# Splitting the prologue's fills over three engines and its LayerNorm into four batches, in a fused attention and GeGLU kernel

## The chip, the cores and the metric

The kernel runs on one core of a Trainium2 chip. The metric is the device time of one execution in microseconds (us). Each kernel was executed several times, and one execution was taken with the hardware profiler. Before the change the three timed executions gave a median of 945.88 us (945.6 to 949.18).

Engines are named as the profile names them: PE is TensorE, PEld its weight loads, ACT is ScalarE, DVE is VectorE, POOL is GpSimd, SP is SyncE, which issues the transfers.

## The reference

```python
x = A_x                                          # [1, 2048, 640], bf16
h = x + attention(layernorm(x), wqkv, wo)        # 32 heads of 20, softmax over 2048 keys
h2 = h + geglu(layernorm(h), w_gate, w_up, w_down)   # inner width 1728
```

The LayerNorm has neither scale nor shift, only (x - mean) / sqrt(var + 1e-5). The softmax needs 32 x 2048 x 2048 exps.

## The kernel before

Nearly all of the time is exps: ScalarE takes most of them, VectorE computes the rest by bit tricks. Ahead of the first exp stands a **prologue**. It loads x, computes the first LayerNorm ("LN1") over 16 tiles of 128 rows, transposes the result on TensorE, projects the first K rows and Q rows, bounds the scores with a maximum over K, and only then starts. This change concerns the prologue.

The program does not write the order of its instructions. It lists operations with a duration, a priority (a smaller number goes first) and what they read and write. A list scheduler in the program turns this into one fixed order for each engine before anything runs:

```python
def op(self, eng, fns, dur, prio, reads=(), writes=(), acq=(), rel=(), after=(), sem=None, lat=None, ...):
...
P_QK, P_PV, P_EPI, P_BG = 0, 1, 2, 3
...
def load(dst, src, key, mb, after=(), writes=None):
    return op("sp", I("dma_start", dst, src), 0.08, P_BG, ..., sem=key, lat=2.2 + mb / 0.25)
```

So `dur` and `lat` are what the scheduler believes. They cost nothing themselves, but a wrong belief gives a bad order, and on the chip an engine stands at the first instruction in its order that can't start: in the run with the fills alone below, TensorE stood 1.94 us at a V matmul, until 17.18, and transposes whose input was ready at 15.98 ran at 19.00.

K and Q are laid out with padding rows that have to be filled first. All the large fills are on Pool:

```python
fills(0, 1, 0, 1)            # K group 0 (1024 words), Q chunk 0 group 0 (256)
... constants ...
fills(1, NG, 0, 1)           # K groups 1 to 7 in one: 7168 words; Q chunk 0: 1792
for c in range(1, 4):        # Q chunks 1 to 3, 2048 words each
    cst(I("memset", qt_all[:, c, :, :]..., 0.0), "qtm%d" % c, 256 * NG)
op("dve", I("memset", PS[:, 512 * 6:512 * 7], 0.0), 0.6, P_QK, ...)
op("dve", I("memset", v_all[:, :, :, DH:DH + 1], 1.0), 0.6, P_QK, writes=["vones"])   # one bf16 in every 21
```

LN1 goes in batches of 4, 4 and 8 tiles. For each tile VectorE takes the statistics (two bn_stats and a bn_aggr). For each batch a few small operations and a square root on ScalarE give the reciprocal deviation. Then each tile is normalised (the "apply"), transposed on TensorE into PSUM (`ps` in the profile), and copied out by ScalarE (the "evacuation"):

```python
for t0, n, eng in ((0, 4, "act"), (4, 4, "act"), (8, 8, "dve")):
    for t in range(t0, t0 + n):
        ln_stats(x_sb[:, t, :], t, [f"x{t // 4}"], P_BG)
    ln_rsqrt(t0, n, P_EPI, True)
    for t in range(t0, t0 + n):
        e_ops.append(ln_apply(eng, x_sb[:, t, :], xn_p[:, t % 4, :], ("xnp", t % 4), t, ...))   # four buffers
        transposes(xn_p[:, t % 4, :], ..., xnT[:, :, t * 128:(t + 1) * 128], ("xnT", t), ALLB, P_EPI, "act")
```

## Time and profile before

| part of the span | us | bounded by |
|---|---|---|
| prologue, to the first exp | 41.46 | LN1, then the K and Q projection |
| exps | 850.18 | ScalarE, busy 842.66 of it |
| tail, from the table load behind the last exps | 52.26 | the last tiles' work, in a chain |
| span | 943.9 | |

The first exp and the tail's table load are read from ScalarE's timeline, and the tail is the difference to the span. Three more lines of the same profile matter later, from VectorE's timeline. The columns are start, duration, engine, line, operation, output and input, and in brackets the idle time before it and what ended that.

```profile
0.98 0.48 DVE L339 MEMSET ps<- 128x512 f32 x1 [0.98 <-PEq L1134]
3.31 0.48 DVE L339 MEMSET v_all<- 128x512 bf16 x1 [1.84 <-issue]
5.14 0.49 DVE L339 BATCH_NORM_STATS2 stats<-rege 128x6 f32<-128x320 bf16 x1 [1.34 <-DMA rege<-in_A_x_dram]
```

The memset of single ones has a gap of 1.84 us in front of it that no wait explains ("issue"). Here it costs nothing, because the statistics wait for x until 5.14 anyway. What the gap is, is worked out with the profile after.

### The profile page before, as it was taken

What the parts mean: (1) busy time and instruction counts of PE and PEld (TensorE: products, weight loads), DVE (VectorE), ACT (ScalarE), POOL (GpSimd) and SP (SyncE); (2) the same over time, 40 slices, a digit from 0 to 9 for tenths busy, and PEclk for the clock granted to TensorE, in tenths of its full rate; (3) what the DMA queues carried; (4) which work ended last, traced back from release to release, by engine and by line L of the source; (5) the groups of instructions that cost most, each with busy time, mean ns of one, the idle gap of its engine ahead of it and who ended that gap; (6) DMA issues with size and microseconds to landing.
All of it is one profiled execution on the core that took longest, in us unless ns stands there. A gap on an engine that the chain in (4) does not pass through costs nothing.

```text
span 943.9 us, 23617 instructions
## 1 busy us (share of the span) xinstructions
PE 852.4 (90%) x10332; PEld 367.6 (39%) x10388; DVE 829.6 (88%) x1804; ACT 881.4 (93%) x789; POOL 17.9 (2%) x26
## 2 busy tenths in 40 slices
PE   2999999998898999998898997999999899999998
PEld 1533232222232223232243333344434446566577
DVE  8849999999799997988799999798999989989953
ACT  3799999999999999999999999999999999999931
POOL 7000000000000000000000000000000000000000
PEclk9999999999999999999999999999999999999999
DMA  7121102325500000001000000001100000000000
GB/s 250 51 73 35 52 15 67 92 59 156 181 1 1 1 1 1 1 15 42 1 3 1 2 1 1 1 2 30 30 1 2 2 15 18 3 17 10 3 22 16
DMA packets 22047, 30.13 MB, mean 32 GB/s; under 512 B 1964, under 2 KB 19464, under 8 KB 21944
## 3 DMA queue, kind: packets, MB, share of 16 engines
q1 hardware_dynamic: 21944, 28.63, 9.8%
q8 instruction: 81, 1.33, 0.6%
q14 instruction: 22, 0.18, 0.1%
HBM read 20.12 MB, written 8.09 MB: 30 GB/s over the span
## 4 chain that ended last, share of the span: by engine, by line
ACT 70%; PE 17%; DVE 12%; issue 0%; DMA 0%; DVEq 0%
ACT pts L339 45%; ACT rege L339 24%; PE ps L592 4%; DVE rege L339 4%; PE ps L1006 4%; PE ps L829 3%; PE ps L339 2%; PE ps L1057 2%; DVE rege L789 2%; DVE qt_all L339 2%; ACT L339 1%; DVE regw L622 1%; DVE stats L339 1%; PE ps L556 1%; DMA rege<-in_A_x_dram 0%
## 5 line engine op out<-in xcount | busy, mean ns | idle before, releaser
L339 ACT ACTIVATE pts<-ps 128x1536 bf16<-128x1536 f32 x480 | 572.2, 1368 | 8.4 <-PE ps L829 5.1
L829 PE MATMUL ps<-qt_all,kt_all 32*128 32x256 bf16 (+2 forms) x3584 | 304.0, 289 | 47.4 <-ACT pts L339 29.2
L339 ACT ACTIVATE rege<-ps 128x1536 bf16<-128x1536 f32 x239 | 298.9, 1369 | 1.7 <-PE ps L339 1.6
L829 PEld LDWEIGHTS ps<-qt_all,kt_all 32*128 32x128 bf16 x3584 | 96.0, 92 | 274.6 <-ACT pts L339 161.4
L339 DVE TENSOR_TENSOR qt_all<-qt_all 128x1024 bf16<-128x1024 bf16 (+1 forms) x240 | 164.1, 684 | 3.2
L1006 PE MATMUL ps<-rege,regw 128*128 128x256 bf16 (+2 forms) x955 | 146.4, 287 | 12.8 <-ACT rege L339 4.8
L339 PE MATMUL ps<-pts,v_all 128*21 128x256 bf16 (+2 forms) x2098 | 138.8, 290 | 0.9 <-DVE rege L339 0.5
L789 DVE TENSOR_SCALAR rege<-ps 128x512 int16<-128x512 f32 x154 | 105.4, 684 | 30.1 <-PE ps L829 29.1
L339 DVE TENSOR_SCALAR qt_all<-qt_all 128x1024 bf16<-128x1024 int16 (+1 forms) x288 | 115.6, 418 | 2.0
L339 PE MATMUL ps<-rege,v_all 128*21 128x256 bf16 (+2 forms) x1294 | 113.3, 292 | 0.0
L1006 PEld LDWEIGHTS ps<-rege,regw 128*128 128x128 bf16 x980 | 72.8, 98 | 63.4 <-issue 21.2
L592 PE MATMUL ps<-regw 128*128 128x320 bf16 (+1 forms) x342 | 81.5, 348 | 3.5 <-ACT regw L562 0.8
L1057 PE MATMUL ps<-regw,rege 128*128 128x320 bf16 x448 | 78.0, 301 | 1.9 <-DVE rege L1046 0.8
L339 PE MATMUL ps<-kt_all,zer 128*32 128x512 bf16 x824 | 70.6, 384 | 0.1
L789 DVE TENSOR_SCALAR qt_all<-ps 128x512 int16<-128x512 f32 x96 | 65.6, 685 | 3.2 <-PE ps L829 2.2
L339 DVE TENSOR_SCALAR rege<-rege 128x1024 int16<-128x1024 int16 (+2 forms) x166 | 67.3, 422 | 1.0
L339 DVE TENSOR_TENSOR rege<-rege 128x1024 bf16<-128x1024 bf16 (+3 forms) x103 | 66.1, 644 | 1.0
L339 PEld LDWEIGHTS ps<-pts,v_all 128*21 128x21 bf16 x2098 | 50.2, 91 | 38.4 <-issue 30.3
L1057 PEld LDWEIGHTS ps<-regw,rege 128*128 128x128 bf16 x448 | 36.9, 98 | 32.6 <-issue 15.2
L339 PEld LDWEIGHTS ps<-rege,v_all 128*21 128x21 bf16 x1294 | 41.1, 91 | 19.8 <-issue 14.3
L592 PEld LDWEIGHTS ps<-regw 128*128 128x128 bf16 x360 | 29.0, 98 | 45.9 <-issue 21.2
L1046 DVE TENSOR_TENSOR rege<-rege,ps 128x512 bf16<-128x512 bf16 (+1 forms) x53 | 35.8, 677 | 10.5 <-PE ps L1006 9.7
(86 smaller groups left out, 611.4 us busy)
## 6 DMA issues: line engine op xcount, KB each, us to landing
rege<-in_A_x_dram SPq DMA_DIRECT2D x6, 640.0 KB, 5.1
q_rows<-regw SPq DMA_DIRECT2D x20, 128.0 KB, 1.7
out_dram<-rege SPq DMA_DIRECT2D x16, 160.0 KB, 2.1
regw<-in_B_w_gate_dram SPq DMA_DIRECT2D x1, 2160.0 KB, 10.4
regw<-in_B_w_up_dram SPq DMA_DIRECT2D x1, 2160.0 KB, 15.4
regw<-in_B_w_down_dram SPq DMA_DIRECT2D x1, 2080.0 KB, 20.6
kt_all<-k_rows SPq DMA_DIRECT2D x12, 160.0 KB
qt_all<-q_rows SPq DMA_DIRECT2D x12, 160.0 KB
```

Source lines behind the costliest of these rows:

```text
L339: return lambda eng: getattr(eng, method)(*args, **kwargs)
L556: op("pe", lambda eng, a=a: eng.transpose(bank16(bk, D)[:, 128 * a:128 * a + 128], src[:, a * 128:(a + 1) * 128], ident[:]), 0.055, prio, ...
L592: yield op("pe", lambda eng, l=l, r=r, k=k: eng.matmul(bank(bk, n), l, r, start=(k == 0), stop=(k == len(steps) - 1)), c_mm(n), prio, mode ...
L622: e = op("dve", lambda eng: eng.tensor_copy(dst, bank(bk)), c_dve(512), prio, reads=[key], writes=[dkey], rel=[bk], after=after)
L789: d_ops.append(op("dve", lambda eng: eng.tensor_scalar(v[:, 512 * h:512 * h + 512], bank(b), EXP_MUL, -32000.0, ALU.mult, ALU.max), c_dve( ...
L829: return lambda eng: eng.matmul(out()[:, kk * nq:(kk + 1) * nq], kt_all[32 * j:32 * j + 32, g, kt * 128:(kt + 1) * 128], qt_all[32 * j:32 ...
L1006: op("pe", lambda eng, a=a, f=f, fi=fi: eng.matmul(bank(bk)[:, fi * nq:(fi + 1) * nq], w[:, a, F0[f]:F0[f] + 128], hnT[:, a, 128 * tb:128 ...
L1046: hdone.append(op("dve", lambda eng, bu=bu, fv=fv, w=w: eng.tensor_tensor(fv, fv, bank(bu, w), ALU.mult), c_dve(w), p, reads=[ku, ("ha", k ...
L1057: op("pe", lambda eng, f=f, o=o, hf=hf, bk=bk: eng.matmul(bank(bk, 320), ha_f[:, o:o + 128], wd[:, f, hf * 320:(hf + 1) * 320], start=(f = ...
```

## The change

The intent is to get the first exp earlier. The padding fills are spread over ScalarE, VectorE and Pool, in the time in which x still arrives, and Pool's are cut into small pieces. LN1 goes in four batches of four. The sums of the second batch are taken by ScalarE as the accumulated outputs of a Copy and a Square; all applies go to VectorE; two evacuations move to VectorE. A priority class P_PRO is added, for LN1 and for the first K and Q rows, and the square roots get a higher priority on ScalarE. Last, the scheduler's beliefs on when the loads land are set to later, more truthful times (also for wo's load and four weight loads under the exps, not shown): V's weights landed at 17.1 us in the runs below, where the old belief was 5.4.

```diff
-P_QK, P_PV, P_EPI, P_BG = 0, 1, 2, 3
+P_QK, P_PV, P_PRO, P_EPI, P_BG = 0, 1, 1.5, 2, 3
...
+        op("act", I("activation", nm[:, 0:1], zer[:, 0:2].bitcast(FP32), ACT.Sqrt), 1.5, P_QK, ...)
+        op("act", I("activation", f32(qt_all[:, 1, :, :]), zer[...].to_broadcast([128, 2048]), ACT.Copy), 1.8, P_QK, ...)
+        op("act", I("activation", f32(qt_all[:, 2, :, :]), zer[...].to_broadcast([128, 2048]), ACT.Copy), 1.8, P_QK, ...)
+        op("dve", I("memset", f32(kt_all[:, 1:4, :]), ones2), 2.9, P_QK, writes=["kf0"])
+        cst(I("memset", kt_all[:, 0, :].bitcast(FP32), ones2), "ktm0", 1024)
...
+        for g in range(4, NG):
+            cst(I("memset", kt_all[:, g, :].bitcast(FP32), ones2), "kf%d" % g, 800)
...
+        for g in range(1, NG, 2):
+            cst(I("memset", f32(qt_all[:, 0, g:min(g + 2, NG), :]), 0.0), "qf0%d" % g, 512)
...
-        fills(1, NG, 0, 1)
-        for c in range(1, 4):
-            cst(I("memset", qt_all[:, c, :, :]..., 0.0), "qtm%d" % c, 256 * NG)
+        for g in range(0, NG, 2):
+            cst(I("memset", f32(qt_all[:, 3, g:g + 2, :]), 0.0), "qf3%d" % g, 512)
...
-                      sem=key, lat=2.2 + mb / 0.25)
+                      sem=key, lat=mb)
-                 f"x{i}", 0.65)
+                 f"x{i}", 5.1 + 1.8 * i)
-        load(wqk, ..., "wqk", 1.6)
-        load(wv, ..., "wv", 0.8)
+        load(wqk, ..., "wqk", 14.0)
+        load(wv, ..., "wv", 16.4)
...
-        for t0, n, eng in ((0, 4, "act"), (4, 4, "act"), (8, 8, "dve")):
+        def act_stats(t0, n):
             for t in range(t0, t0 + n):
-                ln_stats(x_sb[:, t, :], t, [f"x{t // 4}"], P_BG)
-            ln_rsqrt(t0, n, P_EPI, True)
+                for f, k in ((ACT.Copy, 0), (ACT.Square, 1)):
+                    op("act", I("activation", junk, x_sb[:, t, :], f, accum_out=asum[:, k, t - t0:t - t0 + 1]), 0.86, 1.4, ...)
+            ... three small DVE operations turn the sums into mean and variance ...
+        for t0 in (0, 4, 8, 12):
+            if t0 == 4:
+                act_stats(4, 4)
+            else:
+                for t in range(t0, t0 + 4):
+                    ln_stats(x_sb[:, t, :], t, [f"x{t // 4}"], 1.4 if t0 == 12 else P_BG)
+            ln_rsqrt(t0, 4, P_PRO, sqrt=True)
+            for t in range(t0, t0 + 4):
+                e_ops.append(ln_apply("dve", ..., P_PRO))
+                transposes(..., P_PRO, "dve" if t in (13, 15) else "act")
...
-        proj_k(0, PRO, P_EPI, "act")
-        proj_q(0, 0, PRO, P_EPI, "act")
-        q_bound0(PRO, P_EPI)
+        proj_k(0, PRO, P_PRO, "act")
+        proj_q(0, 0, PRO, P_PRO, "act")
+        q_bound0(PRO, P_PRO)
...
-            proj_v(kt, 0, (6, 7), P_BG, "dve")
+            proj_v(kt, 0, (6, 7), P_EPI if kt < 4 else P_BG, "dve")
```

## The prediction

What the recorded texts call a wait for the port, or a port wait, is a VectorE instruction that lasts until a fill of Pool ends. In the profile before, a cast of eight numbers takes 2.73 us and ends at 12.10, as Pool's fill ends at 12.08; after Pool's last fill (19.31) a cast of sixteen takes 0.17. The times are measured. That a shared port is the cause was not shown.

> **What bounds the kernel now.** I read the page's overview first, then the table of engine busy time by stretch, then the timeline of each engine over the first 45 us, and last the waits of ScalarE. The overview has ScalarE (ACT) busy 93% of a 943.9 us span and 70% of the chain that ended last. The stretches say where the other 7% lies:
>
> ```profile
> core 0: us, PE busy (x) PEld busy (x) DVE busy (x) ACT busy (x) POOL busy (x), PEclk, DMA share, GB/s
> 0.00:41.46 41.46, 24.27 (x178) 14.36 (x181) 34.06 (x100) 22.15 (x34) 17.29 (x25) 1.00 0.47 159
> 41.46:100.00 58.54, 56.42 (x431) 18.60 (x437) 44.25 (x94) 58.27 (x52) 0.00 (x0) 1.00 0.19 57
> ...
> 400.00:500.00 100.00, 88.99 (x981) 32.49 (x986) 86.76 (x180) 100.00 (x89) 0.00 (x0) 1.00 0.05 15
> ```
>
> ScalarE is full from 41.46 us, where the first exp starts, to about 892 us, where the last one ends; the hundreds between 100 and 900 us show it busy 97.8 to 100.0 of 100. So the kernel is a prologue of 41.5 us, some 850 us of exps without a real gap, and a tail of about 52 us (the chain of the end has the last exps ending at 891.6 us). The change touches almost only the prologue. The question is therefore one number: how much earlier does the first exp start? Each microsecond there should come off the end, if the exps stay gapless.
>
> In the prologue the VectorE (DVE) timeline shows the loss:
>
> ```profile
> 6.00 6.08 POOL L339 MEMSET kt_all<- 128x7168 f32 x1
> ...
> 9.37 2.73 DVE L339 CAST mv<-mv 128x8 bf16<-128x8 f32 x1
> ...
> 12.13 7.18 POOL L339 MEMSET qt_all<- 128x1792 f32 x4
> 12.14 1.61 DVE L339 TENSOR_SCALAR sd<-mv 128x4 bf16<-128x4 bf16 x1
> ...
> 13.78 0.20 ACT L339 ACTIVATE sd<-sd 128x4 bf16<-128x4 bf16 x1 [11.70 <-DVE stats L339]
> ...
> 17.51 1.83 DVE L339 TENSOR_SCALAR sd<-mv 128x4 bf16<-128x4 bf16 x1
> ```
>
> Columns: start, time, engine, line, operation. A cast of eight numbers takes 2.73 us and ends at 12.10, just as Pool's fill, which began at 6.00, ends (12.08). The same cast takes 0.165 us at 25.25 us, when Pool has finished. And ScalarE does nothing but a table load until 13.78. The later part:
>
> ```profile
> 26.97 1.08 ACT L619 ACTIVATE regw<-ps 128x512 bf16<-128x512 f32 x2
> ...
> 29.20 4.88 ACT L562 ACTIVATE regw<-ps 128x640 bf16<-128x640 bf16 x8 [0.56 <-PE ps L556]
> 33.89 1.17 ACT L619 ACTIVATE regw<-ps 128x512 bf16<-128x512 f32 x2
> 35.47 0.60 ACT L619 ACTIVATE regw<-ps 128x512 bf16<-128x512 f32 x1 [0.41 <-PE ps L592]
> 36.09 1.28 ACT L339 ACT_TABLE_LOAD   x1
> 41.46 3.71 ACT L339 ACTIVATE pts<-ps 128x1536 bf16<-128x1536 f32 x3 [4.09 <-PE ps L829]
> ```
>
> LN1's last eight tiles wait for one late batch of eight. Their evacuations run until 34.1, the fourth K chunk is evacuated at 36.07, then come the maximum over K and the query bound on VectorE and TensorE (5.4 us), then the first exp. The exp table load is hidden in that gap.
>
> [...] the bn_stats keep their 0.44 us during Pool's fill, the cast and the tensor_scalar wait. [...] the trace has 0.70 for the evacuations and 0.913 for the ScalarE applies. [...] The trace has 0.48 us for 512[...].
>
> **The change, part by part.**
>
> *Fills.* Pool's 6.08 us and four 1.6 to 1.8 us fills go. VectorE writes three K groups (3072 words): [...] in a stretch (0.98 to 5.14) where it works 0.97 us in all. With the two old memsets [...] free, but with no slack. ScalarE writes two Q chunks of 2048 words: [...] behind a warm-up Sqrt; also free. Pool keeps pieces of 1024 words (0.95 us seen) and 512 (about 0.55, between 0.31 for 256 and 0.95). By my count of its list, 4.8 us for five K pieces, about 4.8 for the Q pieces and about 4 for the constants, it is done near 14 us instead of 19.3. [...]
> What this takes away on VectorE: the four stuck instructions lost 2.57 + 1.45 + 0.57 + 1.67 = 6.3 us against their free 0.16. What I put back: 1.5 us, some five waits of 0.3.
>
> *LN1.* VectorE loses four tiles of statistics: 4 x 0.86 = 3.4 us (one tile runs from 6.44 to 7.30). It gains eight applies at 0.37 (eight take 2.94 us): 2.9; two evacuations at about 0.4: 0.8; one more root group and three small operations on the sums: about 0.9, less the three products for the negative mean. Sum: -3.4 + 2.9 + 0.8 + 0.8 = +1.1. With the port: -6.3 + 1.5 + 1.1 = -3.7. Smaller batches remove the idle 1.15 us before the last reciprocal and some waits around it, say 1.5: about -5. The last apply, which ends at 31.0 now, should end near 26 to 27.
> ScalarE loses eight applies (7.0 us busy) and two evacuations, and gains eight sum passes of 640 [...] in the stretch from x1's landing to about 14 us that was empty. The x loads take about 1.7 us each (640 KB at about 380 GB/s), so x1 is there near 6.9. From 14 it has 14 evacuations at 0.61 (4.88 for eight), 5 K and Q evacuations at 0.53 and the small roots: 8.5 + 2.7 + 0.6 = 11.8, to about 26. Both engines come out level at 26 to 27, which is the mark of a balanced split, and also means that neither has slack for the other.
>
> *To the first exp.* Last evacuation about 27.5 (34.1 before), fourth K chunk evacuated about 29.5 (36.07). From there to the first exp: 5.4 us before, of which two K evacuations of 0.6 and one V evacuation of 0.4 were interposed in the maximum; the new priority class between attention and epilogue should keep most of them out, so 4.0 to 5.0. First exp near 34, a gain of 7.5; I add 0.5, because the V evacuations that I left in my VectorE count may be put off. About 8 us.
>
> **The rest of the kernel.** The exps, their count and the tail's work stay. But the program order comes from a list scheduler fed with these durations and landing times, so changed loads and keys can reshuffle the whole order. Between 100 and 900 us ScalarE is idle only about 7.3 us in sum, so a reshuffle can gain little there and lose some; the tail may move by 2 us either way. V work no longer done in a shorter prologue goes under the exps, where TensorE is 96% busy, partly with fillers that can give way. So 945.9 - 8 = 938.
>
> **Rivals.** First, *only the wait's place changes*: VectorE stays the bound of the prologue, with port waits at each of the first applies, because they are tensor_scalar and Pool still fills until about 14 us. For it: they are the form that got stuck. Against: pieces are short. Gain then 3 to 5, time 941 to 943. Second, *ScalarE becomes the bound*: if the accumulator costs a further 0.25 us a pass, or Square asks for another table (1.28 us for a load here, twice), evacuations begin 2 to 5 us later. The time is then 940 to 943. Third, *the DMA queue*: SyncE needs 0.74 us an issue (four take 2.96), so eight issues plus landing put the first K and Q rows near 26 if K is ready at 18; that hides, but not if the Q issues stand behind three K chunks. Gain then about 6. Fourth, *full success*: no interposing, all port waits hidden: the first exp at 31, time near 935. Fifth, *wash-out*: the first exp comes early, and ScalarE has new gaps waiting for V or for the second group's K. For it is only TensorE's 96%; against it, the second group's rows are issued by 53.8 us, some 15 us before their use. Time 940 to 945.
>
> **Range and chances.** The centre is 938. The rivals that lose leave 941 to 943, full success with a lucky tail 933. So 933 to 942.5. Faster by 2% would need the end below 927, a gain of 19 us out of a prologue where x lands until 10.3 and the QK weights until 14.6: 0.02. Slower by 2% would take a broken order: 0.01. Within 2%: 0.97.
>
> **What would show it.** In the changed profile: no VectorE instruction of eight numbers above about 1 us; ScalarE busy from about 1 to 14 us; Pool finished near 14; the first evacuation near 14 (16.47 before); the last near 27.5; the first exp between 31 and 36; then a stretch of exps as long as before (850 us) and a tail of about 52. I am wrong if the first exp moves by less than 5 us, if the table is loaded more than once before the exps, or if the exp stretch grows by more than 2 us.

## The result, and the profile after

The four executions of the changed kernel gave 938.92 us in the median (937.99 to 940.96), and the four of the kernel before on the same chip 945.84 (945.6 to 949.18). The ratio is 0.992 (95% interval 0.989 to 0.995). All ratios here are the mean time of one kernel's fast runs over that of the other's fast runs of the same rounds, so not quite the ratio of the medians that are quoted. By the 2% rule the verdict is "same"; against the kernel before alone it is a gain of 7 us.

The profiled execution was the slowest of the four. I took the unchanged changed kernel again in the first experiment job and got a second profile, in an execution of 938.21 us; its four times have a median of 938.39, and the ratio is 0.991 (0.990 to 0.993). The two profiles tell more together than either alone:

| us | before | changed, 1st profile | changed, 2nd profile |
|---|---|---|---|
| first exp starts | 41.46 | 36.40 | 35.22 |
| from there to the tail's table load | 850.18 | 851.05 | 849.48 |
| tail | 52.26 | 51.75 | 51.80 |
| span | 943.9 | 939.2 | 936.5 |

Of the 7.4 us by which the second profile is shorter, 6.24 are the earlier first exp, 0.70 the stretch of exps and 0.46 the tail. The stretches, first profile:

```profile
core 0: us, PE busy (x) PEld busy (x) DVE busy (x) ACT busy (x) POOL busy (x), PEclk, DMA share, GB/s
0.00:36.40 36.40, 21.84 (x154) 12.47 (x154) 30.28 (x97) 24.58 (x45) 12.15 (x32) 1.00 0.54 182
36.40:100.00 63.60, 60.13 (x481) 20.06 (x482) 48.75 (x103) 63.03 (x56) 0.00 (x0) 1.00 0.17 48
...
200.00:300.00 100.00, 91.88 (x791) 27.72 (x788) 94.15 (x213) 98.53 (x88) 0.62 (x1) 0.98 0.32 97
```

The prologue is 5 us shorter, with Pool busy 12.15 us in it and not 17.29. The last line shows where this execution is slower later: the granted TensorE clock was 0.98 there, and ScalarE stood idle for 1.47 us. In the second profile the same hundred has a clock of 1.00 and ScalarE busy 99.92. That is 1.39 of the 1.57 us by which the two stretches of exps differ; that the clock is the cause is likely, but not tested.

**The fills.** VectorE's timeline, first profile:

```profile
1.51 2.62 DVE L339 MEMSET kt_all<- 128x3072 f32 x1 [1.51 <-PEq L1155]
4.23 0.48 DVE L339 MEMSET ps<- 128x512 f32 x1
6.56 0.48 DVE L339 MEMSET v_all<- 128x512 bf16 x1 [1.84 <-issue]
6.66 1.22 DVE L339 BATCH_NORM_STATS2 stats<-rege 128x6 f32<-128x320 bf16 x3
...
10.57 0.15 DVE L339 CAST mv<-mv 128x8 bf16<-128x8 f32 x1
...
11.04 0.15 DVE L339 TENSOR_SCALAR sd<-mv 128x4 bf16<-128x4 bf16 x1
...
21.17 0.18 DVE L339 RECIPROCAL rs<-sd 128x4 f32<-128x4 bf16 x1 [1.32 <-ACT sd L339]
```

The cast of eight numbers takes 0.15 us at 10.57, where the kernel before took 2.73. Pool is then at its small constants, and its fills end at 14.58. The long waits at Pool's fills are gone. But the gap of 1.84 us before the memset of ones has moved. It now follows two other memsets, x has been there since 5.1, and the statistics start at 6.66 and not at 5.14. The last line is a new wait: VectorE stands 1.32 us for a root on ScalarE.

The gap is probably the memset's own time, for the row of a memset seems to begin late. VectorE's first instruction is the memset of 512 words in the kernel before, with a row from 0.98 to 1.46, and the one of 3072 words here, with a row from 1.51 to 4.13. If both began at the same moment (ScalarE's first row is at 0.80 in both), the 2560 further words took 4.13 - 1.46 = 2.67 us, or 1.04 ns each, where the lengths of the rows give (2.62 - 0.48) / 2560 = 0.84. In the same way the memset of ones has a row until 7.04, although the statistics begin at 6.66. From 4.71, where the memset before it ends, to 6.66 it would take about 1.95 us. Both figures are estimates from these rows.

**ScalarE.** Its timeline, first profile:

```profile
2.20 3.69 ACT L339 ACTIVATE qt_all<-zer 128x2048 f32<-128x2048 f32 x2
6.92 0.74 ACT L339 ACTIVATE rege<-rege 128x640 bf16<-128x640 bf16 x1 [1.04 <-DMA rege<-in_A_x_dram]
7.57 0.19 ACT L339 ACTIVATION_READ_ACCUMULATOR rege<-rege 128x1 f32 x1
...
15.67 1.88 ACT L568 ACTIVATE regw<-ps 128x640 bf16<-128x640 bf16 x3
20.45 0.60 ACT L641 ACTIVATE regw<-ps 128x512 bf16<-128x512 f32 x1 [2.90 <-PE ps L614]
20.94 0.29 ACT L339 ACTIVATE sd<-sd 128x4 bf16<-128x4 bf16 x2
...
24.57 4.88 ACT L568 ACTIVATE regw<-ps 128x640 bf16<-128x640 bf16 x8
...
30.82 0.60 ACT L641 ACTIVATE regw<-ps 128x512 bf16<-128x512 f32 x1 [0.39 <-PE ps L614]
31.43 1.28 ACT L339 ACT_TABLE_LOAD   x1
36.40 4.62 ACT L339 ACTIVATE pts<-ps 128x1536 bf16<-128x1536 f32 x4 [3.68 <-PE ps L850]
```

The fills and the sums are as planned, and there is no further table load between 2.09 and 31.43. After the fourth evacuation (17.55) ScalarE stands for 2.90 us, until the first K chunk comes from TensorE. Only behind that evacuation, in ScalarE's fixed order, come the roots of the second and third batch, and VectorE's applies wait for them. TensorE at that time, first profile and then second, each from its own timeline:

```profile
17.05 5.93 PE L614 MATMUL ps<-regw 128*128 128x320 bf16 x21 [0.46 <-ACT regw L568]
```

```profile
17.14 4.66 PE L614 MATMUL ps<-regw 128*128 128x320 bf16 x21 [0.55 <-DMA regw<-in_A_wqkv_dram]
```

The same 21 matmuls (V and K projections) took 5.93 us in one execution and 4.66 in the other. ScalarE, second profile:

```profile
19.73 0.60 ACT L641 ACTIVATE regw<-ps 128x512 bf16<-128x512 f32 x1 [2.19 <-PE ps L614]
...
35.22 4.62 ACT L339 ACTIVATE pts<-ps 128x1536 bf16<-128x1536 f32 x4 [3.68 <-PE ps L850]
```

Up to 17 us the two executions agree to within 0.1 us. Then the K evacuations come 0.72 us (the first) and 1.18 us (the second) earlier, and the first exp 1.18 us earlier.

### The profile page after: what moved, and what is told of

It reads as the page before. It is cut to its first block, busy times and chain, and to the rows that moved or that the text cites. A ratio compares the mean times of both kernels' runs of the same rounds, so it can differ in the third digit from the quotient of the medians.

```text
span 939.2 us, 23514 instructions
## 1 busy us (share of the span) xinstructions
PE 860.0 (92%) x10297; PEld 365.5 (39%) x10297; DVE 829.1 (88%) x1807; ACT 883.7 (94%) x799; POOL 12.8 (1%) x33
## 4 chain that ended last, share of the span: by engine, by line
ACT 77%; PE 15%; DVE 8%; issue 1%; DVEq 0%
ACT pts L339 50%; ACT rege L339 26%; PE ps L1027 4%; PE ps L614 3%; PE ps L850 2%; PE ps L1078 2%; PE ps L339 2%; DVE rege L339 2%; DVE qt_all L339 2%; ACT L339 1%; DVE rege L810 1%; DVE stats L339 1%; PE ps L562 1%; DVE qt_all L810 0%; DVE kt_all L339 0%
## 5 line engine op out<-in xcount | busy, mean ns | idle before, releaser
L1027 PE MATMUL ps<-rege,regw 128*128 128x256 bf16 (+2 forms) x980 | 152.9, 289 | 9.5 <-ACT rege L339 4.3
L810 DVE TENSOR_SCALAR rege<-ps 128x512 int16<-128x512 f32 x154 | 105.5, 685 | 27.5 <-PE ps L850 26.5
L614 PE MATMUL ps<-regw 128*128 128x512 bf16 (+1 forms) x360 | 87.6, 354 | 2.0 <-DVE v_all L747 0.7
L339 PE MATMUL ps<-kt_all,zer 128*32 128x512 bf16 x740 | 65.7, 389 | 0.0
L339 PEld LDWEIGHTS ps<-rege,v_all 128*21 128x21 bf16 x1294 | 41.1, 91 | 19.7 <-issue 13.8
```

The costliest lines, as they stand in the source:

```text
L339: return lambda eng: getattr(eng, method)(*args, **kwargs)
L614: yield op("pe", lambda eng, l=l, r=r, k=k: eng.matmul(bank(bk, n), l, r, start=(k == 0), stop=(k == len(steps) - 1)), c_mm(n), prio, mode ...
L810: d_ops.append(op("dve", lambda eng: eng.tensor_scalar(v[:, 512 * h:512 * h + 512], bank(b), EXP_MUL, -32000.0, ALU.mult, ALU.max), c_dve( ...
L1027: op("pe", lambda eng, a=a, f=f, fi=fi: eng.matmul(bank(bk)[:, fi * nq:(fi + 1) * nq], w[:, a, F0[f]:F0[f] + 128], hnT[:, a, 128 * tb:128 ...
```

## The experiments

Twelve kernels ran, in four jobs; all gave a correct result, and all their executions count as fast. The kernel before was run in the same rounds. Its medians there are 946.7 to 947.5: all its executions with a mean clock of 0.994 to 0.998 took 947.1 us or more, those at 1.000 at most 946.9, and the fastest still lie near 945.6. The theory that I started with: the removed waits at Pool's fills and the new LN1 each give their part of the gain, the fills the larger one. Its rival: LN1's new form does it, and the waits at Pool's fills had hidden something else.

### The change once more

```diff
 # after.py, unchanged
```

> The changed kernel once more, unedited. Its first profile fell in an execution of 940.96 us at a granted clock of 0.998, the other three were 937.99 to 939.05 at 1.0. Theory: the dip of the clock (0.98 between 200 and 300 us) cost that profile some 2 us; a profile at clock 1.0 shows the first exp at 36.4 again and a stretch of exps of about 849 us, and the times have a median of 938 to 939.5. Rival: the 2 us are in the prologue; then the first exp moves to about 34.5 and the stretch stays at 851.

This is the second profile above: median 938.39 us (938.02 to 939.06), ratio 0.991, first exp at 35.22. Theory and rival each hold in part: of the 2.7 us between the two spans, 1.18 lie before the first exp and 1.57 in the stretch of exps. The two profiles set the span of what the change itself does by chance, so the first exps below are compared with both.

### The fills alone

```diff
 # before.py, with the fills of after.py; LN1, priorities and landing times as before
-        fills(0, 1, 0, 1) ... fills(1, NG, 0, 1) ... qtm1 to qtm3 on Pool
+        the ScalarE, VectorE and Pool fills of the change
```

> The kernel before with the new fills alone; LN1, priorities and load times as before. Theory A, [...] the four stuck instructions lose 6.3 us in the kernel before, of which some 2 come back by the later start of VectorE (6.66 instead of 5.14 us), so the first exp comes at 37 to 39 us and the time is 941 to 943.5. Rival B, the new LN1 is what pays: the first exp stays at 40 to 41.5 and the time at 944 to 946.

The median was 946.62 us (ratio 1.000, 0.999 to 1.001), with the first exp at 41.63. The fills alone give nothing. TensorE's timeline shows where their gain went:

```profile
13.71 1.53 PE L563 MATMUL ps<-ident,rege 128*128 128x128 bf16 x10 [13.71 <-ACT rege L339]
17.18 2.02 PE L599 MATMUL ps<-regw 128*128 128x320 bf16 x7 [1.94 <-DMA regw<-in_A_wqkv_dram]
19.00 0.74 PE L563 MATMUL ps<-ident,rege 128*128 128x128 bf16 x5
```

The waits at Pool's fills are indeed gone: the first root runs at 11.70 (13.78 before). But the scheduler believed that the V weights land near 5.4 us (2.2 + 0.8 / 0.25), so it put V matmuls between the transposes. The weights land at 17.1, TensorE stands in order for 1.94 us, and the third tile's transposes, whose input was ready at 15.98, stand behind until 19.00. From there on the run is the kernel before to within 0.2 us (the eight evacuations start at 29.28 and 29.20). My theory fell here: in the kernel before, the waits at Pool's fills lay beside a transfer that ended as late.

### LN1 alone

```diff
 # after.py, with the fills of before.py on Pool (the Sqrt warm-up stays)
-        op("act", ... qf1), op("act", ... qf2), op("dve", ... kf0), Pool's small pieces
+        fills(0, 1, 0, 1) ... fills(1, NG, 0, 1) ... qtm1 to qtm3 on Pool
```

> The changed kernel with the large Pool fills of before (and nothing filled by ScalarE or VectorE). Theory A: casts, roots and now all sixteen applies are in the form that gets stuck while Pool fills, until about 19 us, so the first exp is at 40 to 43 us, no better than before, and the time 943 to 947. Rival B: LN1's four batches carry the gain; first exp at 36.5 to 38, time 939 to 941.

Under this heading LN1 includes the new priorities and the new landing times. The median was 943.1 us (ratio 0.996, 0.995 to 0.998), with the first exp at 40.52. On VectorE's timeline the waits are back, and now they hold the applies too, as my first rival had feared:

```profile
9.28 2.82 DVE L339 CAST mv<-mv 128x8 bf16<-128x8 f32 x1
...
12.13 1.61 DVE L339 TENSOR_SCALAR sd<-mv 128x4 bf16<-128x4 bf16 x1
...
17.72 2.24 DVE L339 TENSOR_SCALAR rege<-rege,mu,rs 128x640 bf16<-128x640 bf16 x2
```

The first exp comes only 0.94 us earlier than before. The rest of the 3.6 us in the median comes from the exps and the tail (about 0.9 us by the profile, span 942.1) and from the runs of before, of which 11 in 24 had a mean clock of 0.996 or 0.998 and took 947.13 us or more. Beside the changed kernel, the fills are worth 4.1 to 5.3 us once LN1 is new (40.52 against 36.40 and 35.22). Each half hides the other's gain.

### No sums on ScalarE

```diff
-            if t0 == 4:
-                act_stats(4, 4)
-            else:
+            if True:
                 for t in range(t0, t0 + 4):
                     ln_stats(...)
```

> The changed kernel with the second batch's statistics on VectorE again (3.4 us more there, 6.9 us less on ScalarE). Theory, VectorE sets the pace of LN1: last apply and first exp 2 to 3.5 us later than in the change (38.4 to 39.9), time 941 to 942.5. Rival, ScalarE's late evacuations set it: the first evacuations come earlier and the first exp stays at 36.4 or earlier, time 939 or less.

The median was 947.6 us (ratio 1.001, 1.000 to 1.002), with the first exp at 42.02: 5.6 to 6.8 us later than with the sums. The direction was expected, the size is about twice as large. Four tiles of statistics are 3.4 us; most of the rest is order, as VectorE's timeline shows:

```profile
27.26 0.44 DVE L745 CAST v_all<-ps 128x320 bf16<-128x320 f32 x1
...
29.23 0.44 DVE L745 CAST v_all<-ps 128x320 bf16<-128x320 f32 x1
...
32.12 1.51 DVE L339 TENSOR_SCALAR rege<-rege,mu,rs 128x640 bf16<-128x640 bf16 x4
```

Between the statistics now stand evacuations of V, six of them between 21.7 and 32.2 us (about 0.4 us each), and the last applies end at 33.6. VectorE sets the pace of LN1. Of the parts that were taken out one at a time, the eight passes on ScalarE cost the most.

### The old landing times

```diff
-                      sem=key, lat=mb)
+                      sem=key, lat=2.2 + mb / 0.25)
 # and each load's size in place of its landing time, as in before.py
```

> The changed kernel with the old landing times in the scheduler's model and nothing else altered. Theory, the order is part of the gain: more V matmuls stand before the first K matmuls, the first K evacuation (19.7 to 20.5 in the change) comes at 21 to 23 and the first exp 1.5 to 4 us later (37 to 40), time 940 to 943. Rival: LN1's four batches make the order indifferent, first exp within 1 us of the change's 35.2 to 36.4, time 938 to 939.5.

The median was 942.78 us (ratio 0.994, 0.993 to 0.996), with the first exp at 38.85: 2.4 to 3.6 us later. The theory held. TensorE's timeline:

```profile
17.19 6.83 PE L614 MATMUL ps<-regw 128*128 128x320 bf16 x33
```

The scheduler, which believes in early V weights, puts 33 matmuls in this run and not 21, so the first K chunk is evacuated at 21.49. I had read this part of the change as bookkeeping.

### The fills and the landing times, LN1 as before

```diff
 # fills_only, and the landing times of after.py
-                      sem=key, lat=2.2 + mb / 0.25)
+                      sem=key, lat=mb)
```

> The kernel before with the new fills and the new landing times of the loads in the scheduler's model, LN1 as before. In fills_only VectorE lost its port waits but TensorE stood 1.94 us at 17.2 us on a V matmul, put between the transposes, until the V weights landed, and ScalarE behind it 2.4 us. Theory: the order assumed weights that were not there, and that wait took the place of the port wait; with the true landing times the matmuls go behind the transposes, the first exp comes at 36.5 to 39.5 us and the time is 940.5 to 944. Rival: the long chain of LN1 itself (sixteen tiles on VectorE, one batch of eight) is the bound, and the first exp stays at 40.5 or later, time 945 to 947.

The median was 946.61 us (ratio 0.9985, 0.997 to 1.000), with the first exp at 40.85, so some 0.8 us better than the fills alone. The V matmuls do go behind the transposes, but another wait takes the place of the one that went. TensorE's timeline, then VectorE's, then ScalarE's:

```profile
17.94 5.08 PE L599 MATMUL ps<-regw 128*128 128x320 bf16 x15
```

```profile
24.45 0.49 DVE L732 CAST v_all<-ps 128x320 bf16<-128x320 f32 x1 [2.52 <-PE ps L599]
```

```profile
26.14 0.20 ACT L339 ACTIVATE sd<-sd 128x8 bf16<-128x8 bf16 x1
...
28.98 4.88 ACT L569 ACTIVATE regw<-ps 128x640 bf16<-128x640 bf16 x8 [0.62 <-PE ps L563]
```

The late batch of eight comes nearly as late as before (28.98 and 29.20), but not because VectorE is still at its work: its statistics of all sixteen tiles end at 21.94. Then it stands for 2.52 us at an evacuation of V, which its order has ahead of the batch's small operations, until TensorE, behind 15 V and K matmuls that take 5.08 us, has done that tile's. So the rival has its number (40.5 or later) and not its reason: this run hangs on the order again, and that LN1's old form is a bound by itself is not shown.

Put together, the first exp (us) by the three parts of the change:

| fills | LN1 and priorities | landing times | first exp |
|---|---|---|---|
| old | old | old | 41.46 |
| new | old | old | 41.63 |
| new | old | new | 40.85 |
| old | new | new | 40.52 |
| new | new | old | 38.85 |
| new | new | new | 36.40, 35.22 |

The fills alone don't gain, and two parts without the new fills, or without the new LN1, gain less than 1 us. The landing times and LN1 were not tried alone.

### The ones on Pool

The gap of 1.84 us before the memset of ones delays the statistics by 1.5 us. Does that delay the first exp?

```diff
-        op("dve", I("memset", v_all[:, :, :, DH:DH + 1], 1.0), 0.6, P_QK, writes=["vones"])
+        cst(I("memset", v_all[:, :, :, DH:DH + 1], 1.0), "vones", 512)
```

> The changed kernel with the fill of V's column of ones moved from VectorE to Pool. VectorE stood 1.84 us before that fill in both kernels; before the change this hid behind x0's landing, after it the first statistics start at 6.66 instead of 5.14. Theory 1, the gap belongs to this strided fill: it goes, the statistics start at 5.1 to 5.3, and the first exp comes 0.8 to 1.5 us earlier, time 937 to 938. Theory 2, the gap belongs to what follows the PSUM fill: the first statistics still start near 6.6 and nothing moves. A rival for the effect: the start moves, but the first exp doesn't, since TensorE waits for the weights (17.1 us) and ScalarE for the first K evacuation.

The median was 939.48 us (ratio 0.991, 0.990 to 0.993), with the first exp at 35.94: between the two profiles of the change. On VectorE the statistics do start at 5.14, but then:

```profile
15.89 1.22 DVE L339 TENSOR_SCALAR mv<-asum 128x4 f32<-128x4 f32 x1
```

Pool's fill of the ones, 2.42 us from 14.67 to 17.09, holds a small VectorE operation until the fill ends (the operation at 17.11). And TensorE waits 1.52 us for the V weights, again until 17.08, and again takes long for its 21 matmuls (5.45 us), so the first K chunk is evacuated at 20.46. The fill of single ones is slow on either engine (2.42 us on Pool, some 1.95 on VectorE by the estimate above); the 1.5 us lost on VectorE are real, but they lie beside a transfer, and the 21 matmuls behind it were slow here as in the first profile. The third rival of the expectation was right.

### A warm TensorE

The two profiles of the change differ by how fast TensorE runs its first 21 matmuls, 5.93 and 4.66 us. I call a matmul of 512 cold where it is recorded with 0.63 us and warm where it is recorded with 0.38; the first of that width among the 21 are cold. TensorE's first work in both profiles is transposes, from 13.59. The theory was that a run of matmuls before those would make the 21 warm, and that the cold start costs the 1.2 us between the two first exps. To test it, TensorE gets 18 matmuls without use, while LN1's first statistics run:

```diff
                     ln_stats(x_sb[:, t, :], t, [f"x{t // 4}"], 1.4 if t0 == 12 else P_BG)
+                    if t == 0:
+                        wbk = Bank(7)
+                        op("pe", [I("matmul", PS[:, 512 * 7:512 * 8], ident[:], kt_all[:, 0, 0:512], ...)] * 18, 5.5, P_QK,
+                           mode="full", reads=["ident", "ktm0", ("mv", 0)], acq=[wbk], rel=[wbk])
```

> The changed kernel with 18 matmuls of 512 columns into an unused bank before the first transpose, started when the first tile's statistics are done; their result is never read. In the two profiles of the change the first K matmuls of 512 took 0.63 us each for a while (three of them in one profile, about a dozen in the other) and 0.38 later, and the first exp differed by 1.2 us (36.40, 35.22), as did the first K evacuation (20.45, 19.73, then 21.99, 20.81). Theory: [...] warmed up, all K matmuls take 0.38, the first K evacuation comes at 18.3 to 19.3 and the first exp at 33.5 to 35, time 936.5 to 938. Rival: they are slow for another reason, such as the weights still landing, and nothing moves; or the first exp hangs on VectorE alone and only the K evacuation moves.

The median was 937.9 us (937.83 to 939.29; ratio 0.990, 0.988 to 0.991), with the first exp at 34.86. The theory held. A narrow cut of TensorE's timeline at the same moment, first the first profile of the change and then this run:

```profile
18.07 1.06 PE L614 MATMUL ps<-regw 128*128 128x512 bf16 x2
```

```profile
18.08 0.82 PE L619 MATMUL ps<-regw 128*128 128x512 bf16 x3 [0.28 <-ACT regw L568]
```

Three matmuls take less than two did. A single one is recorded with 0.38 us when warm, so the distance from start to start is (0.82 - 0.38) / 2 = 0.22 us here; the cold ones are recorded with 0.63, so (1.06 - 0.63) / 1 = 0.43. The 18 useless matmuls take 6.47 us together, from 8.05 to 14.52, and five of them start before 10.00. If they are cold first and warm after, that is an estimated 11 steps of 0.43 and 6 of 0.22 us (4.73 + 1.32, and 0.38 for the last: 6.43), so they turned warm after some 4.7 us of work. The weights land as before (TensorE waits for V's until 17.10), so they are not what made the matmuls slow. The clock column of the profile does not show this state: it reads 1.00 from 17 to 20 us of the first profile too, where these matmuls are 0.43 us apart. The first K chunk is evacuated at 19.37, and the wait before it is 1.34 us and not 2.90 (0.48 of the difference only because the useless matmuls delay the four evacuations before it, which end at 18.03 and not at 17.55):

```profile
19.37 0.60 ACT L646 ACTIVATE regw<-ps 128x512 bf16<-128x512 f32 x1 [1.34 <-PE ps L619]
...
34.86 4.62 ACT L339 ACTIVATE pts<-ps 128x1536 bf16<-128x1536 f32 x4 [3.68 <-PE ps L855]
```

It has the lowest median of the study. Against the change it is ahead by 0.5 to 1.0 us in the medians; the two weren't timed in the same rounds and the intervals of their ratios overlap, so only the earlier first exp is shown, in one profile, not that margin.

### The roots before the later statistics

In the change the root of the second batch waits until VectorE has taken all the statistics (19.7 us). Here it gets the higher priority:

```diff
-            d = lambda fn, r, w: op("dve", fn, 0.17, P_EPI, reads=r, writes=w)
+            d = lambda fn, r, w: op("dve", fn, 0.17, 1.3, reads=r, writes=w)
...
-                    ln_stats(x_sb[:, t, :], t, [f"x{t // 4}"], 1.4 if t0 == 12 else P_BG)
+                    ln_stats(x_sb[:, t, :], t, [f"x{t // 4}"], P_BG)
```

> The changed kernel with two priorities altered: the sums and the root of the second batch go ahead of the statistics of the third and fourth. In the change ScalarE's sums are done at 15.8 us, but the three small operations on them stand between later bn_stats (16.65, 17.97, 18.28), the second batch's first apply comes at 20.7 to 21.4, and ScalarE then has all its last ten evacuations in one row until 28.3 to 29.5. Theory: with the batches in order, the second batch's applies start at 17 to 19, ScalarE spreads its evacuations, the last one ends 1 to 2 us earlier and so does the first exp (33.5 to 35), time 936.5 to 938. Rival: VectorE has the same total of work before the last apply, so the last batch is as late as before and the first exp stays at 35 to 36.5.

The median was 944.04 us (ratio 0.996, 0.995 to 0.998), with the first exp at 38.43, so later. The theory fell. VectorE's timeline:

```profile
20.28 1.50 DVE L339 TENSOR_SCALAR rege<-rege,mu,rs 128x640 bf16<-128x640 bf16 x4
23.19 1.77 DVE L339 TENSOR_SCALAR rege<-rege,mu,rs 128x640 bf16<-128x640 bf16 x4 [1.41 <-PE ps L562]
...
25.68 0.48 DVE L339 BATCH_NORM_STATS2 stats<-rege 128x6 f32<-128x320 bf16 x1
```

The four applies of the second batch start earlier (20.28, against 21.39 and 20.67), but there are only four buffers for normalised tiles. The next four wait until TensorE has transposed, and TensorE is at its slow V and K matmuls (20 of them, 17.07 to 22.87). The last statistics stand behind those applies in VectorE's order, and the last batch's root comes at 27.3.

### K and V later

After the maximum over K, TensorE and VectorE do work for the second group and for V that the first exp doesn't need. Here all of it is made to wait for the first query bound, but for the first half of the first four V tiles:

```diff
-      [("xnT", tt) for tt in range(4 * c, 4 * c + 4)] + ["wqk"], prio))
+      [("xnT", tt) for tt in range(4 * c, 4 * c + 4)] + ["wqk"] + ([("qo", 0, 0)] if ("qo", 0, 0) in sc.lw else []), prio))
...
-      [("xnT", kt), "wv"], prio))
+      [("xnT", kt), "wv"] + ([("qo", 0, 0)] if kt >= 4 or hf else []), prio))
```

> The changed kernel with the second to fifth K and Q groups and all V tiles but the first four (first half) held back until the first group's query bound is written. Between the last K evacuation and the first exp lie 4.98 us in the change, in which three K evacuations (0.69) and two V evacuations (0.49) of VectorE are interposed. Theory: without them this takes 3.3 to 4.2 us and the first exp comes 0.8 to 1.7 us earlier. What is held back goes under the exps; if TensorE has room there (96% busy, partly with fillers) the stretch of exps stays within 1 us of 849.5 and the time is 937 to 938. Rival, wash-out: the stretch grows by 1 us or more, as V or the second group is late, and the time is 938.5 or more.

The median was 949.87 us (ratio 1.003, 1.002 to 1.004): slower than before, although the first exp came at 34.54. From the end of the last K evacuation to the first exp it took 4.26 us (30.28 to 34.54) and not 4.98. But the stretch of exps grew to 861.8 us, by 12.3 over the second profile of the change. ScalarE's timeline, and then TensorE's:

```profile
57.58 1.02 ACT L339 ACTIVATE pts<-ps 128x1024 bf16<-128x1024 f32 x1 [4.60 <-PE ps L339]
```

```profile
53.88 3.11 PE L614 MATMUL ps<-regw 128*128 128x320 bf16 x20
56.92 0.39 PE L339 MATMUL ps<-pts,v_all 128*21 128x512 bf16 x2
```

The V matmuls stand in front of the matmuls that consume the exps, and ScalarE waits for those (in the stretch of exps it is idle for 19.0 us against 7.1). This is the wash-out rival of the prediction, brought about on purpose.

### Four edits together

```diff
 # after.py with the ones on Pool, 14 warm-up matmuls, the roots first, and K and V later
```

> The changed kernel with the four edits together: ones on Pool, TensorE warmed up (14 matmuls), batches in order, later K, Q and V held back. If their gains on the first exp add (0 to 0.5, 1, 1 to 2, 1 us) it comes at 31.5 to 33.5 us and the time is 934.5 to 936.5. If the prologue has another bound behind them (the V and QK weights landing at 17.1 and about 14.6, and the work of VectorE), the first exp stays at 33.5 to 34.5 and the time at 937 or more.

The median was 953.13 us (ratio 1.006, 1.004 to 1.009), with the first exp at 37.44 and a stretch of 861.8 us. The gains don't add; the late first exp of the root order and the long stretch of K and V later both come through.

### Warm, and the ones later

```diff
 # warm_pe, and
-        op("dve", I("memset", v_all[:, :, :, DH:DH + 1], 1.0), 0.6, P_QK, writes=["vones"])
+        op("dve", I("memset", v_all[:, :, :, DH:DH + 1], 1.0), 2.3, P_BG, reads=[("qo", 0, 0)], writes=["vones"])
-        load(wqk, ..., "wqk", 14.0)
-        load(wv, ..., "wv", 16.4)
+        load(wqk, ..., "wqk", 14.7)
+        load(wv, ..., "wv", 17.4)
```

> The changed kernel with TensorE warmed up as in warm_pe, V's column of ones filled by VectorE after the query bound of the first group instead of before LN1, and the landing times of the two weight loads in the model set to what the profiles show (QK 14.7, V 17.4 instead of 14.0, 16.4), which puts the first K matmuls ahead of the V matmuls. Theory: the first statistics start at 5.1 to 5.3, no Pool fill is in the way after 14.6 (in ones_on_pool the fill moved to Pool held VectorE until 17.1), the second batch's applies start near 18.8 (20.3 in warm_pe) and the first exp comes at 32.8 to 34.2 (34.86 in warm_pe); with a stretch of exps of about 849.5 and a tail of 51.8 the time is 935.5 to 937.5. Rival: the new order under the exps costs more than the prologue gains, as in k1_late, or the late fill of the ones holds up the first VectorE exps: the stretch is 851 or more and the time 938 or more.

The median was 942.58 us (ratio 0.995, 0.994 to 0.997). The first exp was the earliest of all, 34.42, but the stretch of exps is 856.0 us, with ScalarE idle for 12.8 us of it (7.1 in the warm kernel). Its timeline has one such wait:

```profile
96.00 2.36 ACT L339 ACTIVATE pts<-ps 128x1536 bf16<-128x1536 f32 x2 [1.55 <-PE ps L339]
```

Between 55 and 96 us there are five of these, 4.6 us together, all for TensorE. The rival held. The waits have the form of those with K and V later, so V work under the exps is the likely cause, but this was not followed further, and which of the two edits does it, the later ones or the later landing times, was not separated.

## Why the prediction was right or wrong

The predicted 938.0 us lies within the changed kernel's executions (937.99 to 940.96), and "within 2%" was right. The steps under it did less well.

**The prologue decides: right.** ScalarE was busy 842.4 to 842.7 us in the stretch of exps in all three profiles; what moved was the start. "Each microsecond there should come off the end, if the exps stay gapless" held for the change, and the condition is the important half: in the run with K and V later the first exp came early and 12 us were lost behind it.

**Waits at Pool's fills lose 6.3 us, 1.5 put back: the waits went as foreseen, the sum was not additive.** The stuck instructions went to 0.15 us each (the casts from 2.73 and 0.73, the tensor_scalars from 1.61 and 1.83). What was put back is smaller than 1.5: the first batch's four applies take 1.65 us (0.39 + 0.51 + 0.75) against 1.51 for four later ones, and nothing small stuck. But the fills alone gave 0.0 us: TensorE then waited for the V weights until 17.18, and where the order was put right (the fills and the landing times), VectorE waited 2.52 us at an evacuation of V and the gain was 0.6. I had listed "a transfer that is hidden anyway" for the K and Q rows, and not for the V weights that the scheduler had put between the transposes.

**VectorE's fill, "free, but with no slack": right for the fill, wrong for what stands behind it.** By the estimate from the ends of the rows the fill took some 3.2 us (3072 x 1.04 ns), though its row shows 2.62. But I had counted the memset of the ones with the 0.48 us of its row, and with the gap before it, it takes about 1.95 by the same estimate. Before the change that was hidden behind x; now the statistics began at 6.66 and not at 5.14. This cost little: with the start at 5.14 again, in the ones on Pool, the first exp was 35.94, between the two profiles of the change.

**Last apply at 26 to 27: about right** (26.66 and 25.58), with errors that partly cancel. The late start cost 1.5 us and the new wait for a root 1.32 and 0.61, and I had neither. Against that, the waits at Pool's fills were 1.4 us less than I put back, and three V evacuations and a K evacuation that stood before the last apply (24.39 to 28.0, some 1.8 us) went behind it.

**ScalarE from 14 to 26 without gaps, last evacuation at 27.5: the step that failed.** It came at 29.45 and 28.28. From the first evacuation (14.35) to that end ScalarE was busy for 10.73 us and idle for 4.37: 2.90 before the first K evacuation, 0.76 before the second, 0.71 before the next transposes. In the second profile the same waits are 2.19 + 0.29 + 0.71 = 3.19. I had added work and no waits. The roots stand behind the K evacuation in ScalarE's order, and K waits for matmuls of which the first are cold (0.43 us apart); with the matmuls warm (0.22) the first of these waits is 1.34. Not all of such a wait reaches the first exp, as VectorE is at its statistics until 19.84. What reaches it is VectorE's wait for the root: 1.32, 0.61 and 0.25 us in the two profiles and the warm run, with the first exp at 36.40, 35.22 and 34.86. So by these waits a warm TensorE has little more to give, and why the warm run still lies 0.9 us above 34 was not tested.

**Fourth K evacuation at 29.5, K to exp 4.0 to 5.0.** It ended at 31.42 and 30.24, 1.97 us after the last evacuation as foreseen (2.0), and from there it took 4.98 both times, at the edge of the range. The new priority class was to keep evacuations out of the maximum over K, and they are still there (in the first profile V at 31.36 and 32.47, K at 33.12 and 34.34); held back in the run with K and V later, they left 4.26. Summed up for the first profile: 34 + 1.95 (last evacuation) - 0.03 (1.97 in place of 2.0) + 0.48 (4.98 less 4.5, the middle of the range) = 36.40.

**First exp near 34, a gain of 7.5 plus 0.5: mis-sized.** It measured 36.40 and 35.22, gains of 5.06 and 6.24, just above the 5 that would have been "wrong". In the second profile a shorter stretch of exps (0.70) and a shorter tail (0.46) made up for most of the difference. I had counted these as unknown, plus or minus 2, so the time came out right partly by luck.

**Rivals.** "Only the wait's place changes" is what the fills alone show, and with the old fills the applies do get stuck (two take 2.24 us, where four take 1.51 elsewhere). "ScalarE becomes the bound" through the accumulator or a table load: no. A pass with its accumulator read comes every 0.86 us, and there is one table load before the one for exp. "The DMA queue": for the K and Q rows nothing of it is seen, as the first exp waits for TensorE (3.68 us). "Full success" at 31 was reached in no run: the earliest first exp is 34.42. "Wash-out" did not happen to the change, but it is close by.

**Readings.** The cast at 25.25 us that I called "the same" has sixteen numbers, not eight; with 0.17 us for more numbers it makes the same point. TensorE's 96% is read from the stretch of 41.46 to 100 us; in the hundreds from 100 to 900 it is busy 87.5 to 94.8.

**What stays open.** Why the later K and V order costs 12 us and not less was followed to the waits for V, not to the scheduler's choice. How the two tails differ by 0.46 us was not looked into.

## What to carry to other kernels

A removed wait is worth something only if what it stood beside is also over: before counting it, look at what every engine in the chain waits for at the same moment, above all at transfers that a static order was built around. In a prologue of several engines, add the waits between them and not only the work, and look how far apart TensorE's first matmuls start (here 0.43 and then 0.22 us for a matmul of 512). If the first are slow, useless matmuls while TensorE has nothing to do are worth a run: here the first exp came at 34.86 with them, and at 36.40 and 35.22 without. And an earlier start is a gain only while the work that was in front of it isn't moved under the stretch that is already full.

## What single instructions cost here

- A memset on VectorE seems to take longer than its row shows. The rows of 512 and 3072 words are 0.48 and 2.62 us long, while their ends lie 2.67 us apart for 2560 words: an estimated 1.04 ns each, if both began at the same moment.
- The memset of 512 single bf16, one in every 42 bytes, shows 0.48 us on VectorE like a dense one, with 1.84 to 1.91 us before it that no wait explains, wherever it stands (after a memset, or at 35.7 us in the run with the ones later); on Pool it shows as 2.42 us, where 512 dense fp32 words took 0.60 (four in 2.41). That the gap goes with this memset is shown by the two runs that move it; why it takes so long was not shown.
- The accumulator output of an ACTIVATE is a second instruction in the profile, recorded with 0.19 us; a pass of 640 with it repeats every 0.86 us.
